# Identity products, three moves between engines and a new order in a pooled-attention and gated-MLP kernel

## The chip, the cores and the metric

The kernel runs on one core of a Trainium2 chip. The metric is the device time in microseconds, as the median of three runs. Five things work side by side on the core: TensorE (PE, with its weight loads as PEld), VectorE (DVE), ScalarE (ACT), GpSimd (POOL) and the DMA queue that SyncE (SP) feeds. Each engine takes its own instructions strictly in the order in which the program wrote them, and waits on semaphores for the others.

## The reference

Three layers follow one another. Batch is 8, with 8 heads, 576 positions and a head size of 64.

```python
def _attn_ref(q, k, v):
    k_p = k.reshape(B, H, S // 8, 8, D).mean(axis=3)      # pooled keys
    v_p = v.reshape(B, H, S // 8, 8, D).mean(axis=3)      # pooled values
    scores = scale * np.matmul(q, k_p.transpose(0, 1, 3, 2))
    scores = scores - np.max(scores, axis=-1, keepdims=True)
    attn = np.exp(scores)
    attn = attn / (np.sum(attn, axis=-1, keepdims=True) + 1e-09)
    return np.matmul(attn, v_p)

def _moe_ref(x, w_in, conv_w, w_out):                     # 512 -> 1024 -> 512
    h = np.maximum(x @ w_in, 0.0)
    conv_out = sum(conv_w[k] * shifted(h, k) for k in range(3))
    return (h * sigmoid(conv_out)) @ w_out

def _moe2_ref(x, w_in, g_ln, w_sg, b_sg, w_out):          # 512 -> 2 x 512 -> 512
    u, v = split(gelu_tanh(x @ w_in))
    v_n = (v - mean(v)) / np.sqrt(var(v) + 1e-06) * g_ln
    v_s = np.einsum('ts,bsd->btd', w_sg, v_n) + b_sg[None, :, None]
    return x + (u * v_s) @ w_out
```

## The kernel before

Every large product is computed from operands split into a high and a low part, each rounded for fast matmuls: three products per pair (high by high, low by high, high by low). The high part is written by ACT as a cast (`hi`), the low part by a subtraction in `subtract` (line 135), on DVE or POOL.

**What sets the order.** The work is written as small generators (`t_k`, `t_s`, `t_v2` and so on), and a long string `ORDER` lists which of them advances by one `yield` at each step. The function `step` also ties each instruction to the one before it on its engine, so the string alone fixes the order on all five queues. A token such as `s2.1` is task `s`, part 2, batch 1.

**The stages.** (1) The start, to about 55 us: the keys and values of batch 0 are loaded and pooled over eight rows, q is transposed through PE and an ACT copy (`qT`), the scores come from `KBT` (the pooled keys, L423), DVE takes the maximum and subtracts it (L434, L436), ACT does the exponential, DVE the sum and its reciprocal, POOL scales (`en`, L453, L457), PE transposes (L483, L492), ACT and DVE write the split parts `eTh` and `eTl`. The attention products (`t_a`, through `passes` at L776) read these and the pooled values `Vh`, `Vl`, `VR`, and ACT writes the rows `xh` and `xl` of the first MLP. Ident, the 128x128 identity, is made by POOL at the very start. (2) To about 540 us: hidden slices `t_i` (L106, twelve matmuls each into a `psi` bank, then ACT and DVE: L567, L577, L579, L580, L582, L586) and their output products `t_o`, with the attention of later batches between them. (3) To about 735 us: the input product of the second MLP in a form with seven products of quarter blocks instead of eight (`t_v2`, `t_u`, `t_xc`); `t_v2` ends with the normalisation of v (statistics on DVE, L813 and L814; 1/sqrt on POOL, L817 and L818; subtract and multiply on DVE, L821) and a store to `vs`. (4) To the end: per batch, `vs` is read back, sums and splits `sc` are made (POOL at L957, ACT at L626, DVE at L135), the remaining 64 rows become `vr` (L965), the spatial products `t_sp` run, DVE adds (L1006), POOL multiplies by u (L1010), and the last product `t_o2` (L99 to L101) adds the residual.

**Banks.** `psi` is a ring of two PSUM banks (`i_bank`), `psa` of three, `pso` of three. The two `psi` banks carry the hidden slices, the scratch of weight conversions (`to_f32`, L147, L150, L153) and the last products.

**Pooling the first keys.** `t_k(i, b)` pools blocks of 128 rows (two per step, 64 rows in the last). For batch 0, steps 0 and 2 are one DVE reduction each (L251), and step 1 is three additions on POOL (L253, L255, L257). `t_kfin` then transposes the five pooled blocks `kp` by PE (L294) into `KBT`.

Of the kernel before, what the change touches and what calls it, by code (L numbers as in the profile page):

```python
# [11 lines left out]
AF = mybir.ActivationFunctionType  # L12
ALU = mybir.AluOpType
# [13 lines left out]
def pooled_attention_gated_mlps(  # L27
# [23 lines left out]
    nc = tc.nc  # L51
# [15 lines left out]
    REM = S - NM * 128  # L67
# [24 lines left out]
    def i_bank():  # L92
        return psum1.tile([128, 512], F32, tag="i", bufs=2, name="psi")
# [40 lines left out]
    def subtract(out, in0, hi, eng=nc.vector):  # L134
        eng.tensor_tensor(out=out, in0=in0, in1=hi.bitcast(F32), op=ALU.subtract)  # L135
# [125 lines left out]
    def t_k(i, b):  # L261

        n = (2, 2, 1)[i]
        P = 128 if i < 2 else 64
        if b > 1:
            raw = att2.tile([128, 2, 512], F32, tag="raw", name="raw")
        else:
            raw = staged(f"st{b}", n, ((in1, "xh", XW * KC), (slot, "hg", 2 * NF * CH))[b] if i == 0 else None)
        rows_ = k[b].rearrange("h (j r) d -> (h j) (r d)", r=POOL)[256 * i:256 * i + P * n]
        nc.sync.dma_start(out=raw[0:P, 0:n], in_=rows_.rearrange("(a p) x -> p a x", p=P))  # L270
        if b == 1:
            kv["k1", i] = raw
        yield
        if b == 1:
            return
        if ("kp", b) not in kv:
            kv["kp", b] = att1.tile([128, 5, D], F32, tag="kp", name="kp")
        eng = dve if b == 0 and i != 1 else pool
        yield from pool_sum(eng, raw[:, 0:n], kv["kp", b][0:P, 2 * i:2 * i + n, :], P)
# [502 lines left out]
    def t_v2(a, k):  # L782
# [37 lines left out]
        for j in range(2):  # L820
            nc.vector.tensor_scalar(out=vg[:, j, :], in0=vg[:, j, :], scalar1=mv[:, j, 0:1], scalar2=rs[:, j:j + 1],  # L821
                                    op0=ALU.subtract, op1=ALU.mult)
# [108 lines left out]
    def t_w_out2(i, *_):  # L931
        p, tag = ((slot, "w4"), (slot, "w6"), (w2["q"], "T3"), (w2["q"], "T4"))[i]
        return weight(p, tag, w_out2[128 * i:128 * i + 128, :], dve, i_bank, lambda hl: wo2.__setitem__(i, hl))
# [28 lines left out]
    def t_vr(_, b):  # L962
        x = vf[b, 0][:, 2]
        r = vrs[b] = w2["p"].tile([128, HF], F32R, tag=f"b{1 + b % 2}", name="vr")
        nc.scalar.copy(out=r, in_=x)  # L965
        yield
        subtract(r[REM:128], x[REM:128], r[REM:128])
# [161 lines left out]
```

## Time and profile before

| what | us |
|---|---|
| three runs | 942.87, 940.72, 941.30 (median 941.3) |
| profiled execution: device time | 941.96 |
| profiled execution: span from the first to the last instruction | 940.2 |
| PE busy in the span | 915.5 (97%) |
| DVE busy | 757.6 (81%) |
| POOL busy | 558.0 (59%) |
| ACT busy | 534.6 (57%) |
| mean granted TensorE clock | 0.993 of full speed |

How to read it: a row of a timeline gives the start and the duration in us, the engine, the line of the kernel, the operation, the tile written and the tiles read, the shape and the count of merged instructions; in brackets stands the idle time of the engine just before it and what ended that. A row of windows gives a stretch, its length, the busy time and the number of instructions of PE, PEld, DVE, ACT and POOL, then the granted TensorE clock (1.00 is 2.4 GHz, 0.50 is 1.2 GHz), the busy share of the DMA engines and GB/s. A row of groups gives line, engine, operation, tiles and shapes, the count, and after the bar the busy time in us, the mean duration in ns, and the idle time before them with its releasers. PE's durations overlap, since matmuls are pipelined: the spacing of starts is the cost of one.

### The profile page before, as it was taken

Reading aid. Unit: us, or ns where it says so; the run is one execution under the profiler, and the core shown is the slowest. Engines: PE = TensorE matmul, PEld = TensorE weight load, DVE = VectorE, ACT = ScalarE, POOL = GpSimd, SP = SyncE. Lnnn points to the kernel's source line nnn. Section 1 sums busy time; section 2 is a strip of 40 time slices with the busy share of each in tenths; the row PEclk is TensorE's granted clock in tenths of the full one; section 3 lists DMA queues with packets and bytes.
Section 4 is the critical chain, followed back from the end, with each engine's and each line's share of the span. In section 5 each row is a group of like instructions: output and inputs, shape, how many; then the busy total and the mean of one; then the engine's idle time right before and its main releaser. Section 6 shows DMA issues by size and latency. Waiting matters only on the chain.

```text
span 940.2 us, 15870 instructions
## 1 busy us (share of the span) xinstructions
PE 915.5 (97%) x5412; PEld 839.1 (89%) x5412; DVE 757.6 (81%) x1383; ACT 534.6 (57%) x1125; POOL 558.0 (59%) x630
## 2 busy tenths in 40 slices
PE   5899999999999999999999999999999999999998
PEld 4797889989898898998998899999999998998996
DVE  5789988888977697797688778898787988888764
ACT  3766777767767576667646657656666422323211
POOL 3686797886878666457326456643563654555421
PEclk9799999999999999999999999999999999999999
DMA  9974384755645535323353474556536745476644
GB/s 236 247 208 101 107 177 126 168 152 153 168 124 134 134 102 125 106 73 105 92 131 85 88 161 133 153 186 197 141 134 219 263 149 197 151 208 196 182 163 134
DMA packets 185901, 143.62 MB, mean 153 GB/s; under 512 B 106048, under 2 KB 140124, under 8 KB 185820
## 3 DMA queue, kind: packets, MB, share of 16 engines
q1 hardware_dynamic: 185820, 142.61, 55.6%
q8 instruction: 42, 0.69, 0.3%
q14 instruction: 39, 0.32, 0.1%
HBM read 94.20 MB, written 48.37 MB: 152 GB/s over the span
## 4 chain that ended last, share of the span: by engine, by line
PE 86%; DVE 7%; ACT 2%; DMA 2%; issue 1%; SPq 0%; POOL 0%; DVEq 0%; ACTq 0%; POOLq 0%
PE psi L106 21%; PE psa L776 17%; PE pso L776 13%; PE pso L99 7%; PE pso L101 7%; PE pso L100 7%; PE psa L423 4%; PE psi L101 3%; PE psi L99 3%; PE psi L100 3%; PE psa L106 1%; DMA vf<-vs 1%; DVE sc L135 1%; DVE mx L434 1%; DMA q<-in_q_dram 1%
## 5 line engine op out<-in xcount | busy, mean ns | idle before, releaser
L135 POOL TENSOR_TENSOR hg<-g,hg 128x384 fp32r<-128x384 f32 x96 | 99.9, 1049 | 70.7 <-ACT hg L589 69.8
L1010 POOL TENSOR_TENSOR u<-u,tmp 128x288 f32<-128x288 f32 x64 | 60.4, 966 | 61.5 <-DVE tmp L1006 61.3
L579 DVE SCALAR_TENSOR_TENSOR psi<-h,coef,psi 128x384 f32<-128x384 f32 x96 | 58.9, 614 | 37.6 <-ACT psi L577 37.0
L582 ACT ACTIVATE psi<-psi 128x384 f32<-128x384 f32 x96 | 45.8, 478 | 51.9 <-DVE psi L580 51.5
L567 ACT ACTIVATE h<-psi 128x386 f32<-128x386 f32 (+1 forms) x96 | 47.4, 494 | 47.7 <-PE psi L106 47.3
L717 POOL TENSOR_TENSOR xb<-xb 128x768 f32<-128x768 f32 x24 | 45.4, 1892 | 43.6 <-DVE xc L135 27.6
L135 POOL TENSOR_TENSOR eTl<-xb,eTh 128x512 fp32r<-128x512 f32 (+1 forms) x30 | 45.4, 1513 | 39.1 <-ACT eTh L507 31.1
L586 DVE SCALAR_TENSOR_TENSOR g<-psi,h 128x384 f32<-128x384 f32 x96 | 52.2, 546 | 14.8 <-ACT psi L582 12.8
L626 ACT CAST sc<-vf 128x512 fp32r<-128x512 f32 x48 | 28.9, 619 | 61.3 <-POOL vf L957 35.2
L580 DVE SCALAR_TENSOR_TENSOR psi<-h,coef,psi 128x384 f32<-128x384 f32 x96 | 59.8, 623 | 3.4
L589 ACT CAST hg<-g 128x384 fp32r<-128x384 f32 x96 | 48.0, 508 | 24.3 <-DVE g L586 24.1
L577 ACT ACTIVATE psi<-h,coef 128x384 f32<-128x384 f32 x96 | 56.3, 586 | 3.1
L423 PE MATMUL psa<-KBT,qT 128*128 128x144 f32 (+1 forms) x320 | 52.5, 296 | 3.0 <-ACT qT L405 1.3
L423 PEld LDWEIGHTS psa<-KBT,qT 128*128 128x128 f32 (+1 forms) x320 | 44.3, 182 | 10.1 <-issue 4.0
L776 PE MATMUL pso<-wc,xc 128*128 128x256 f32 x378 | 50.9, 283 | 1.0 <-ACT tmp L799 0.9
L776 PEld LDWEIGHTS pso<-wc,xc 128*128 128x128 f32 x378 | 48.5, 189 | 1.9 <-ACT tmp L799 1.6
L776 PE MATMUL psa<-wc,xc 128*128 128x256 f32 x378 | 50.0, 282 | 0.0
L776 PE MATMUL psa<-xc,wc 128*128 128x384 f32 x252 | 48.2, 338 | 0.9 <-ACT tmp L843 0.9
L776 PEld LDWEIGHTS psa<-wc,xc 128*128 128x128 f32 x378 | 48.4, 189 | 0.2
L776 PE MATMUL pso<-xc,wc 128*128 128x384 f32 x252 | 47.8, 337 | 0.0
L135 DVE TENSOR_TENSOR sc<-vf,sc 128x512 fp32r<-128x512 f32 x48 | 41.2, 869 | 8.0 <-ACT sc L626 8.0
L1025 ACT CAST g<-u 128x256 fp32r<-128x256 f32 x64 | 22.6, 403 | 42.3 <-POOL u L1010 39.3
(403 smaller groups left out, 3110.3 us busy)
## 6 DMA issues: line engine op xcount, KB each, us to landing
xb<-eds SPq DMA_DIRECT2D x24, 384.0 KB, 3.4
x2s<-ob SPq DMA_DIRECT2D x36, 256.0 KB, 2.3
us<-ub SPq DMA_DIRECT2D x24, 384.0 KB, 3.3
vs<-vg SPq DMA_DIRECT2D x18, 512.0 KB, 3.1
u<-us SPq DMA_DIRECT2D x16, 576.0 KB, 6.7
vf<-vs SPq DMA_DIRECT2D x16, 512.0 KB, 3.8
out_dram<-ob SPq DMA_DIRECT2D x32, 256.0 KB, 2.0
xb<-x2s SPq DMA_DIRECT2D x40, 192.0 KB, 4.1
```

Source lines behind the costliest of these rows:

```text
L99: nc.tensor.matmul(out=out_, lhsT=ah, rhs=bh, start=first, stop=False)
L100: nc.tensor.matmul(out=out_, lhsT=al, rhs=bh, start=False, stop=False)
L101: nc.tensor.matmul(out=out_, lhsT=ah, rhs=bl, start=False, stop=last)
L106: nc.tensor.matmul(out=out_, lhsT=a, rhs=b_, start=(i == 0), stop=(i == n - 1))
L135: eng.tensor_tensor(out=out, in0=in0, in1=hi.bitcast(F32), op=ALU.subtract)
L423: nc.tensor.matmul(out=ps[0:n, 2 * SP * x:2 * SP * x + 2 * SP], lhsT=qT[:, p, 0:n], rhs=KBT[:, p, :], start=True, stop=True)
L577: nc.scalar.activation(out=y, in_=tap(1), func=AF.Copy, scale=cw(1, f))
L579: nc.vector.scalar_tensor_tensor(out=y, in0=tap(0), scalar=cw(0, f), in1=y, op0=ALU.mult, op1=ALU.add)
L580: nc.vector.scalar_tensor_tensor(out=y, in0=tap(2), scalar=cw(2, f), in1=y, op0=ALU.mult, op1=ALU.add)
L586: nc.vector.scalar_tensor_tensor(out=go, in0=y, scalar=1.0, in1=tap(1), op0=ALU.add, op1=ALU.mult)
L776: nc.tensor.matmul(out=ps, lhsT=a, rhs=b_, start=first and i == 0, stop=last and i == n - 1, skip_group_check=True)
L1010: pool.tensor_tensor(out=z, in0=z, in1=o, op=ALU.mult)
```

## The change

Five things change. Lines after the first edit stand 3, 12 or more higher in the new kernel (L423 becomes L426, L776 becomes L779, L1010 becomes L1022).

1. In the pooling of batch 0's keys, step 1 is split: one of its two blocks is a DVE reduction, the other stays three additions on POOL, of half the size.
2. A new task `t_turn` (token X) takes a `psi` bank and multiplies the identity by itself; nothing reads the result. There are 37.
3. The subtractions of the four weights of the last product (`t_w_out2`), and those of `vr` for batches 0 and 1, go from DVE to POOL.
4. In the last block (k = 5) and for its second and third part, the normalisation runs on ACT as scale and bias, and POOL makes the bias in two more instructions on two columns. `t_v2` has one more `yield` for all parts.
5. `ORDER` is another list.

```diff
-ORDER = '''z k0.0 k1.0 k2.0 z z p0.0 c p1.0 ...
+ORDER = '''z k0.0 k1.0 k2.0 z z p0.0 c p1.0 ...
...
         eng = dve if b == 0 and i != 1 else pool
+        if b == 0 and i == 1:
+            yield from pool_sum(dve, raw[:, 1:2], kv["kp", b][:, 3:4, :], P)
+            n = 1
         yield from pool_sum(eng, raw[:, 0:n], kv["kp", b][0:P, 2 * i:2 * i + n, :], P)
...
-        for j in range(2):
-            nc.vector.tensor_scalar(out=vg[:, j, :], in0=vg[:, j, :], scalar1=mv[:, j, 0:1], scalar2=rs[:, j:j + 1],
-                                    op0=ALU.subtract, op1=ALU.mult)
+        if k == NBLK - 1 and a:
+            pool.tensor_tensor(out=mv[:, :, 0], in0=mv[:, :, 0], in1=rs, op=ALU.mult)
+            pool.tensor_scalar(out=mv[:, :, 0], in0=mv[:, :, 0], scalar1=-1.0, scalar2=None, op0=ALU.mult)
+            yield
+            for j in range(2):
+                nc.scalar.activation(out=vg[:, j, :], in_=vg[:, j, :], func=AF.Identity, scale=rs[:, j:j + 1],
+                                     bias=mv[:, j, 0:1])
+        else:
+            yield
+            for j in range(2):
+                nc.vector.tensor_scalar(out=vg[:, j, :], in0=vg[:, j, :], scalar1=mv[:, j, 0:1],
+                                        scalar2=rs[:, j:j + 1], op0=ALU.subtract, op1=ALU.mult)
...
-        return weight(p, tag, w_out2[128 * i:128 * i + 128, :], dve, i_bank, lambda hl: wo2.__setitem__(i, hl))
+        return weight(p, tag, w_out2[128 * i:128 * i + 128, :], pool, i_bank, lambda hl: wo2.__setitem__(i, hl))
...
-        subtract(r[REM:128], x[REM:128], r[REM:128])
+        subtract(r[REM:128], x[REM:128], r[REM:128], pool if b < 2 else dve)
...
+    def t_turn(*_):
+        ps = i_bank()
+        nc.tensor.matmul(out=ps[:, 0:128], lhsT=ident, rhs=ident, start=True, stop=True)
```

The new order shows at three places. The first is DVE at the start; `kp` is the pooled keys, `st` the loaded ones, `cf` the filter taps. Before:

```order
L251 TENSOR_REDUCE kp<-st_139 128x128
L251 TENSOR_REDUCE kp<-st_139 64x64
L147 TENSOR_SCALAR cf<-craw 24x128
L300 COPY KBT<-psa 64x3x72
L303 COPY KBT<-psa 64x64
```

Now:

```order
L251 TENSOR_REDUCE kp<-st_139 128x64
L251 TENSOR_REDUCE kp<-st_139 128x128
L251 TENSOR_REDUCE kp<-st_139 64x64
L147 TENSOR_SCALAR cf<-craw 24x128
L303 COPY KBT<-psa 64x3x72
L306 COPY KBT<-psa 64x64
```

The new reduction of the half block, whose keys are loaded second, stands ahead of the block that is loaded first.

The second is PE from the small products of the filter taps (L188) to the first attention product (L776, now L779), some 26 to 35 us into the run. Before:

```order
L188 MATMUL psa<-ident,cf 128x28
L106 MATMUL psa<-q_148,ident 64x64 x8
L401 MATMUL psa<-ident,q_148 128x64 x4
L483 MATMUL psa<-ident,en 128x128 x4
L423 MATMUL psa<-KBT,qT 64x144 x2
L492 MATMUL psa<-ident,en 32x128 x2
L401 MATMUL psa<-ident,qb 128x128 x4
L423 MATMUL psa<-KBT,qT 64x144 x2
L776 MATMUL psa<-eTh,Vh 128x288
```

Now:

```order
L106 MATMUL psa<-q_148,ident 64x64 x8
L1086 MATMUL psi<-ident 128x128 x3
L404 MATMUL psa<-ident,q_148 128x64 x4
L486 MATMUL psa<-ident,en 128x128 x4
L404 MATMUL psa<-ident,qb 128x128 x4
L1086 MATMUL psi<-ident 128x128
L426 MATMUL psa<-KBT,qT 64x144 x2
L495 MATMUL psa<-ident,en 32x128 x2
L1086 MATMUL psi<-ident 128x128
L426 MATMUL psa<-KBT,qT 64x144 x2
L1086 MATMUL psi<-ident 128x128 x2
L779 MATMUL psa<-eTh,Vh 128x288
```

The transposes of the next batch's q (`qb`) stand one group earlier, ahead of the scores that wait for `qT`, and seven identity products stand between the rest. Of the 37, eleven open PE's queue, fifteen lie between the first transposes and the end of the first attention products, one lies among the hidden slices, and ten lie where stage 3 turns into stage 4.

The third is POOL at that turn, near 739 to 753 us; `u` is the tile that t_sp multiplies, `vr` the 64 remaining rows, `T3hl` and `T4hl` two weights of the last product. Before:

```order
L957 TENSOR_TENSOR vf<-sf,vf 128x2x256
L1010 TENSOR_TENSOR u_8231<-u_8231,tmp_8565 128x288
L1010 TENSOR_TENSOR u_8581<-u_8581,tmp_8614 128x288
L1010 TENSOR_TENSOR u_8231<-u_8231,tmp_8673 128x288
L1010 TENSOR_TENSOR u_8581<-u_8581,tmp_8683 128x288
L1010 TENSOR_TENSOR u_8231<-u_8231,tmp_8565 128x288
L1010 TENSOR_TENSOR u_8581<-u_8581,tmp_8614 128x288
L957 TENSOR_TENSOR vf<-vf 128x2x256
```

Now:

```order
L1022 TENSOR_TENSOR u_8394<-u_8394,tmp_8695 128x288
L1022 TENSOR_TENSOR u_8441<-u_8441,tmp_8631 128x288
L1022 TENSOR_TENSOR u_8394<-u_8394,tmp_8738 128x288
L1022 TENSOR_TENSOR u_8441<-u_8441,tmp_8760 128x288
L1022 TENSOR_TENSOR u_8394<-u_8394,tmp_8695 128x288
L1022 TENSOR_TENSOR u_8441<-u_8441,tmp_8631 128x288
L135 TENSOR_TENSOR vr<-vf,vr 64x512
L1022 TENSOR_TENSOR u_8394<-u_8394,tmp_8714 128x288
L1022 TENSOR_TENSOR u_8441<-u_8441,tmp_8690 128x288
L135 TENSOR_TENSOR T4hl<-t,T4hl 128x512
L969 TENSOR_TENSOR vf<-vf 128x2x256
L135 TENSOR_TENSOR T3hl<-t,T3hl 128x512
```

Three subtractions have come between the products with u.

## Rows read from the trace of the kernel before

**Rows 1.** The page: busy us per engine; a group: count, busy us, mean ns.
```profile
PE 915.5 (97%) x5412; PEld 839.1 (89%) x5412; DVE 757.6 (81%) x1383; ACT 534.6 (57%) x1125; POOL 558.0 (59%) x630
...
L586 DVE SCALAR_TENSOR_TENSOR g<-psi,h 128x384 f32<-128x384 f32 x96 | 52.2, 546 | 14.8 <-ACT psi L582 12.8
```

**Rows 2.** Windows: length, busy us (count) of PE, PEld, DVE, ACT, POOL; clock; DMA.
```profile
80.00:100.00 20.00, 19.06 (x111) 15.84 (x110) 18.82 (x38) 14.72 (x34) 13.44 (x19) 1.00 0.61 143
...
720.00:740.00 20.00, 17.84 (x136) 17.04 (x135) 18.12 (x37) 9.95 (x21) 13.69 (x12) 1.00 0.85 275
```

**Rows 3.** Timeline of PE, its start: start us, us, line, operands, count [idle before].
```profile
8.89 1.09 PE L401 MATMUL psa<-ident,q 128*128 128x128 f32 x4 [8.89 <-DMA q<-in_q_dram]
9.77 1.30 PE L294 MATMUL psa<-ident,kp 128*64 128x128 f32 x5
...
14.21 0.63 PE L401 MATMUL psa<-ident,q 128*128 128x128 f32 x4
...
15.92 2.02 PE L106 MATMUL psa<-st,ident 128*128 128x128 f32 x16
```

**Rows 4.** Timeline of DVE and POOL, the pooling of batch 0's keys.
```profile
4.87 1.87 DVE L251 TENSOR_REDUCE kp<-st 128x128 f32<-128x1024 f32 x1 [3.26 <-DMA st<-in_k_dram]
...
6.88 1.26 POOL L253 TENSOR_TENSOR st<-st 128x512 f32<-128x512 f32 x1 [4.10 <-DMA st<-in_k_dram]
...
7.84 1.01 DVE L251 TENSOR_REDUCE kp<-st 64x64 f32<-64x512 f32 x1 [1.10 <-DMA st<-in_k_dram]
...
9.02 0.45 POOL L257 TENSOR_TENSOR kp<-st 128x128 f32<-128x128 f32 x1
```

**Rows 5.** Windows of 5 us where the granted clock falls.
```profile
25.00:30.00 5.00, 3.54 (x33) 2.91 (x33) 4.76 (x11) 3.97 (x14) 4.20 (x9) 0.98 1.10 236
30.00:35.00 5.00, 4.52 (x17) 3.32 (x18) 4.27 (x10) 3.34 (x8) 4.04 (x9) 0.50 1.11 176
35.00:40.00 5.00, 4.24 (x18) 3.54 (x16) 3.36 (x6) 2.92 (x7) 4.42 (x4) 0.50 1.11 216
```

**Rows 6.** Timeline of PE from 28 to 48 us.
```profile
30.48 1.22 PE L423 MATMUL psa<-KBT,qT 128*64 128x144 f32 x4 [1.28 <-ACT qT L405]
...
34.58 0.45 PE L776 MATMUL psa<-eTl,Vh 128*128 128x288 f32 x1
34.82 0.45 PE L776 MATMUL psa<-eTh,Vl 128*128 128x288 f32 x1
...
47.31 0.30 PE L776 MATMUL psa<-eTh,Vl 128*128 128x288 f32 x1
47.45 0.29 PE L776 MATMUL psa<-eTh,VR 96*128 96x288 f32 x1
```

**Rows 7.** Timeline of POOL, what gates the first attention products.
```profile
31.94 1.26 POOL L135 TENSOR_TENSOR VR<-vrm,VR 32x512 fp32r<-32x512 f32 x1 [0.71 <-ACT VR L367]
...
43.39 1.20 POOL L453 TENSOR_TENSOR en<-e,rs 64x256 f32<-64x256 f32 x2 [3.52 <-ACT xl L540]
```

**Rows 8.** Timeline of DVE in the third stage of batch 0.
```profile
98.29 1.30 DVE L408 STREAM_TRANSPOSE qT<-qb 128x512 f32<-128x512 f32 x2
```

**Rows 9.** Groups, 700 to 770 us: shapes, count, busy us, mean ns, idle before.
```profile
L821 DVE TENSOR_SCALAR vg<-vg,mv,rstd 128x512 f32<-128x512 f32 x10 | 5.0, 540 | 0.9 <-POOL rstd L818 0.9
...
L818 POOL TENSOR_TENSOR rstd<-rstd,small 128x2 f32<-128x2 f32 x5 | 4.3, 852 | 0.4
...
L808 ACT ACTIVATE vg<-vg 128x512 f32<-128x512 f32 x4 | 2.5, 633 | 2.6 <-DVE vg L804 2.6
...
L135 DVE TENSOR_TENSOR vr<-vf,vr 64x512 fp32r<-64x512 f32 x2 | 1.5, 756 | 0.1
```

**Rows 10.** Timeline of DVE near 750 us.
```profile
749.61 0.69 DVE L135 TENSOR_TENSOR T3hl<-t,T3hl 128x512 fp32r<-128x512 f32 x1 [0.20 <-ACT T3hl L211]
```

**Rows 11.** Timeline of PE, the longest wait after 120 us.
```profile
738.77 1.06 PE L776 MATMUL pso<-sgp,sc 128*128 128x288 f32 x6 [1.56 <-DVE tmp L1006]
```

**Rows 12.** Timeline of POOL in the same stretch.
```profile
738.84 6.45 POOL L1010 TENSOR_TENSOR u<-u,tmp 128x288 f32<-128x288 f32 x6
```

More of the change, by code (lines that the diff above doesn't have):

```diff
@@ L1069, in t_o2 @@
                 nc.sync.dma_start(out=out[r0:r0 + REM, :], in_=ob[REM * e:REM * e + REM])
-    tasks = {"z": t_setup, "c": t_coef, "i": t_w_in, "t": t_w_out, "k": t_k, "K": t_kfin, "v": t_v, "V": t_vfin,
+    def t_turn(*_):
+        ps = i_bank()
+        nc.tensor.matmul(out=ps[:, 0:128], lhsT=ident, rhs=ident, start=True, stop=True)
+    tasks = {"X": t_turn, "z": t_setup, "c": t_coef, "i": t_w_in, "t": t_w_out, "k": t_k, "K": t_kfin, "v": t_v, "V": t_vfin,
              "q": t_q, "p": t_qtr, "s": t_s, "e": t_e, "x": t_x, "h": t_hg, "a": t_a, "I": t_i, "O": t_o, "A": t_att_close,
```

2 lines of the change are left out of this document (1 added, 1 removed).

## The prediction

> **What bounds the kernel now.** I read the page first: PE is busy 915.5 of the 940.2 us of the span [rows 1], so nearly all of the time is PE's own queue, and a gain can only come from PE's idle time or from time in which its clock is low. I then went through the windows and the timeline of PE to see where either lies. There are four places.
>
> The first is the start. PE does nothing for 8.89 us, until the first q has landed, and its first products are slow: four transposes start at 8.89 and the next group at 9.77, 0.22 us each, against 0.63 us for four at 14.21 [rows 3]. The second is the stretch from 30 to 40 us. PE idles 1.46 us from 25 to 30 us, 1.28 of it in one gap that ends at 30.48 with ACT's copy of `qT`, and then the granted clock is 0.50, the lower of its two levels (1.2 GHz), for both of the next windows [rows 5, 6]. The same attention product goes from a spacing of 0.24 us (34.58 to 34.82) to one of 0.14 us (47.31 to 47.45) when the clock is back at 1.00 (2.4 GHz) [rows 6]. The third is the stretch behind it, where DVE is the full engine: from 80 to 100 us it is busy 18.82 of 20 us and PE idles 0.94 us [rows 2]. The fourth is the turn from stage 3 to stage 4: from 720 to 740 us PE idles 2.16 us, 1.56 of it in one wait for DVE's `tmp`, with DVE at 18.12 of 20 [rows 2, 11]. Between 120 and 600 us PE hardly idles, and the end of the program has the same tasks in the same sequence as before.
>
> **The change part by part.** The sums are made against the profiled execution (941.96 us); the median of the three runs is 0.66 us lower, and that is taken off at the end.
>
> *Pooling by halves.* POOL's three additions for two blocks run from 6.88 to 9.47 us [rows 4]. Half of that leaves POOL ready about a microsecond earlier. But DVE now takes the half block first, and its keys land at 6.88, when POOL could start [rows 4]; a block of 512 elements per row costs 1.01 us, the pair that DVE used to take at 4.87 costs 1.87, the last block 1.01 [rows 4]. DVE thus ends at 6.88 + 1.01 + 1.87 + 1.01 = 10.77, and the first pair is ready at 9.76, where the pooled-key transposes started at 9.77 anyway [rows 3]. Only the fifth transpose waits for 10.77, and the copy that everything waits for needs the first four. I take 0, with +0.6 as the bad end (the fifth transpose holds up the queue).
>
> *Eleven identity products ahead of the data.* A 128x128 product of this type costs 2.02 / 16 = 0.13 us at the high level [rows 3]. Eleven at the low level of 0.22 are 2.4 us, and need only the identity, so they end near 4 us, well before 8.89, and delay nothing. If they leave the clock high, the early groups gain: the two groups of four transposes 0.4 us each; at most 0.9 us. The row shows that after idleness PE begins slow [rows 3], and some five microseconds of idleness still lie between these products and the data. So I take 0, with -0.9 as the other end. The Trainium skill, "TensorE: Matmul & The Clock Gate" (Part 1, What's actually happening), says that the throttled state is the default, that activity releases it and that idleness brings it back; that speaks against these eleven. The trace agrees as far as it goes: the slow first products follow 8.89 us without work. By that page this term is 0, by the other reading -0.9.
>
> *Fifteen among the first tiles.* At 0.13 us they are 1.9 us. PE idles 2.70 us from 25 to 40 us alone (5 - 3.54, 5 - 4.52, 5 - 4.24) [rows 5], and the new order has seven of the fifteen there. Since they depend on nothing late they fill gaps; some will end up ahead of work that was ready. I take +0.4, between 0 and 1.9.
>
> *The clock from 30 to 40 us.* This is the main term. The three identity products and the transposes of `qb` (4 x 0.16 [rows 3]) now stand before the scores that waited until 30.48, so about 1.0 us of the gap that came just before the fall is filled. If the clock stays high, PE's 8.76 us of work in those two windows [rows 5] becomes 4.38: 4.4 us is the most. But POOL gates the first attention product with `VR`, which ends at 31.94 + 1.26 = 33.20 [rows 7] whatever the clock does. Of the ten microseconds 6.8 lie behind that; less the 0.76 idle of the second window, half of 6.0 is 3.0 us. What is late next is ACT, which writes each `xh` before the next product can go on, and I give 0.5 back for it. The scaled scores of the last tile can follow: POOL waited 3.52 us for them at 43.39 [rows 7], so POOL has room. I take -2.5, between 0 and -4.4.
>
> *The turn.* DVE loses the four normalisations of two parts (540 ns each, 2.2 us), two `vr` subtractions (756 ns each, 1.5) [rows 9] and, near 750 us, two weight subtractions (0.69 each, 1.4) [rows 10]: 5.1 us of an engine that is full there. PE's idle 2.16 us there [rows 2] is the most that this can return; I take 1.6, since some of it is PE's own chain. Ten identity products at 0.13 cost 1.3 on PE's queue there. Net -0.3, between +1.3 and -0.9. ACT takes the normalisations; the nearest row is a 128x512 activation of 633 ns [rows 9], so four are 2.5 us on an engine that is busy 9.95 of 20 us there [rows 2], and they feed rows that only the last two batches read: nothing on the path. Of the two subtractions moved that lie near 640 us, I take 0, since neither DVE nor POOL sets PE's pace there for long. POOL gets four subtractions of 512 columns (1.26 us each by the nearest row [rows 7]) and four small ones of at most 0.85 us each [rows 9]; what that can do is a rival.
>
> *The rest.* One identity product among the hidden slices: +0.13. The new order elsewhere: 0, from -0.9 (the idle of 80 to 100 us goes [rows 2]) to +2.7 (second rival). Sum: -2.5 + 0.4 + 0.1 - 0.3 = -2.3; 941.96 - 2.3 - 0.66 = **939.0 us**.
>
> **The rivals.** *The clock falls all the same, one step later.* With the gap before 30.48 filled, the next thin place is the one ahead of `VR`: two groups of scores (1.22 us each at the low level [rows 6], 0.6 at the high), two small transposes and four identity products until 33.20, some 2.0 us of work in 2.7. If the clock falls there, it is low for the attention products just as before, and the main term is 0: 941.96 + 0.4 + 0.1 - 0.3 - 0.66 = 941.5. For it speaks that POOL's queue up to `VR` has the same instructions in the same sequence in both orders; against it that the work that stood before the fall was thinner still.
>
> *DVE work pulled ahead: slower.* In the new order DVE has 190 instead of 187 instructions ahead of the filter taps of the eleventh hidden slice: one more pooling (1.01 us [rows 4]), one more transpose of q (1.30 / 2 = 0.65 [rows 8]) and one more gating product (0.55 [rows 1]); at the third slice it is two maxima and two subtractions more. The difference is 2.2 us there and up to 2.7 with the shapes that changed, and nearly gone by the fifteenth. DVE is full in that stretch and PE already waits for it [rows 2]. It decides as soon as DVE's queue reaches 60 us without having gained as much as it was given; if the clock term is lost too, the whole sum is 941.96 + 0.2 + 2.7 - 0.66 = 944.2.
>
> *POOL binds at the turn.* POOL multiplies six times without a break from 738.84 to 745.29 [rows 12]; the second `vr` stands behind these six, then the two weights. By my count PE reaches the products with that `vr` about when POOL ends it (745.3 + 1.3), so each microsecond that POOL comes late is one that PE waits. Then the gain of 1.6 is gone: 939.0 + 1.6 = 940.6. The Trainium skill, "GPSIMD Engine Reference" (section 4.1, Engine selection), advises against two-input elementwise work on GpSimd as about half as fast as VectorE. The rows agree: 1.26 against 0.69 to 0.76 us for 512 columns [rows 7, 9, 10].
>
> *More than forecast.* The clock is high from the first data on (-0.9), the whole 3.0 is kept, the idle of 80 to 100 us goes (-0.9) and the turn gives its best (-0.9): 941.96 - 5.7 + 0.1 - 0.66 = 935.7.
>
> **How the numbers follow.** The forecast gets 0.43, the later fall 0.23, DVE 0.13, the larger gain 0.13, POOL 0.08. The forecast's own range is 937.0 to 940.4. The range that should hold 8 in 10 runs from 935.0, a little under the larger gain, to 943.0, which leaves most of the DVE rival out. About 0.2%, 1.9 us, is what a measurement of this kernel can tell from no change. Faster than 939.4: 0.38 of the forecast, all of the larger gain and a little of the later fall, 0.55. Slower than 943.2: 0.11 of DVE and 0.03 of the later fall, 0.14. The rest, 0.31, is the same.
>
> **What would show it.** In the windows after, the granted clock from 30 to 45 us: 1.00 throughout makes the main term right, 0.50 from about 33 us makes the first rival right. The first transposes near 8.9 us: four in 0.9 us or in 0.6. The first hidden slice should start 2 to 3 us earlier than before. PE's idle from 60 to 120 us tells whether DVE gave the gain back. From 720 to 740 us, PE's wait for `tmp` should be gone and no wait for POOL in its place. The prediction is wrong if PE idles somewhere between 120 and 700 us, where I counted the new order at nothing.

## The result: 0.95% slower, and the profile after

| | median us | runs | ratio to the kernel before, 95% interval |
|---|---|---|---|
| kernel before, beside it | 942.09 | 4 (940.72 to 943.89) | 1 |
| changed kernel | 950.98 | 4 (950.44 to 952.19) | 1.0095 [1.0074, 1.0116] |

The forecast was 939.0 us, with a range to 943.0. The profiled execution of the changed kernel took 952.19 us, its span 950.4.

The page of the changed kernel, busy time by engine (to set against [rows 1]):

```profile
PE 928.1 (98%) x5486; PEld 852.7 (90%) x5486; DVE 758.9 (80%) x1374; ACT 539.4 (57%) x1129; POOL 565.8 (60%) x640
```

PE's idle time is smaller than before: 950.4 - 928.1 = 22.3 us against 940.2 - 915.5 = 24.7. But the eleven products now fill part of the wait at the start: up to its first transposes PE idles 3.1 us (1.38 + 1.72) where it idled 8.89 [rows 3]. Behind them it idles 19.2 us against 15.8. The rest of the loss is in PE's *busy* time: 74 more matmul records (37 products, two records each), and products that run at half speed. Windows of the changed kernel (length, busy us and count of PE, PEld, DVE, ACT, POOL, granted clock, DMA share, GB/s); the first three answer to [rows 5]:

```profile
25.00:30.00 5.00, 4.36 (x43) 3.83 (x42) 4.79 (x9) 4.20 (x15) 4.04 (x10) 1.00 1.10 213
30.00:35.00 5.00, 4.63 (x34) 3.75 (x33) 4.16 (x10) 4.22 (x9) 4.19 (x6) 1.00 1.10 220
35.00:40.00 5.00, 2.40 (x18) 1.93 (x18) 1.13 (x3) 1.80 (x6) 4.08 (x7) 0.99 1.07 214
40.00:47.00 7.00, 7.00 (x41) 6.45 (x40) 5.57 (x10) 3.19 (x12) 1.45 (x3) 0.52 1.06 373
...
115.00:120.00 5.00, 3.18 (x14) 3.18 (x15) 3.71 (x7) 1.81 (x4) 3.15 (x4) 0.84 0.88 214
120.00:125.00 5.00, 4.50 (x17) 4.15 (x16) 3.07 (x7) 4.06 (x10) 1.98 (x3) 0.50 0.15 52
```

The clock is at 1.00 from 30 to 40 us (0.99 in the second half), where the kernel before had 0.50: that part of the forecast came true. But there are two new holes, 35 to 40 us (PE busy 2.40 of 5) and 115 to 120 us (3.18 of 5), and behind each of them the clock is at its lower level for some 7 us.

How far the changed kernel is behind can be read from start times: for every product that both traces have with the same operands, its start after less its start before. The medians by place of the trace before, for the kernels of this document (one trace of each, worked out from the rows of PE; in us, negative is ahead):

| place, us | 20-40 | 40-60 | 60-80 | 100-120 | 120-140 | 200-220 | 320-340 | 340-360 | 700-720 | 760-780 |
|---|---|---|---|---|---|---|---|---|---|---|
| changed kernel | -0.3 | 2.1 | 2.5 | 2.7 | 7.0 | 7.0 | 7.8 | 9.1 | 9.3 | 10.6 |
| e4, without products | -0.3 | 2.0 | 2.3 | 2.4 | 5.3 | 5.4 | 6.2 | 7.5 | 7.1 | 7.4 |
| e3, two entries moved | -0.2 | -3.2 | -0.9 | -0.8 | -1.0 | -0.9 | -0.1 | 1.2 | 1.1 | 2.2 |
| e5, e3 without products | 0.0 | -3.3 | -1.4 | -1.6 | -1.6 | -1.5 | -0.7 | 0.6 | 0.2 | 1.0 |
| e9, e5 with four more moved | 0.0 | -2.9 | -1.2 | -1.1 | -1.1 | -1.1 | -1.3 | -0.8 | -1.1 | -1.2 |
| e7, before with the moved work | -0.2 | -2.3 | -2.1 | -2.1 | -2.1 | -2.1 | -2.3 | -2.3 | -2.3 | -0.3 |
| e12, before with products in its waits | -0.5 | -2.5 | -2.4 | -2.3 | -2.3 | -2.3 | -2.5 | -2.5 | -2.6 | -2.2 |

Seven of the nine microseconds are lost by 130 us, in two steps that sit behind the two holes. Here is the first hole: one row of POOL in the kernel before, then rows of POOL, ACT and PE of the changed kernel:

```profile
29.34 0.11 POOL L519 MEMSET xl<- 128x8 f32 x1
```

```profile
34.06 1.30 POOL L135 TENSOR_TENSOR wi1hl<-t,wi1hl 128x512 fp32r<-128x512 f32 x1
35.31 1.29 POOL L135 TENSOR_TENSOR wi0hl<-t,wi0hl 128x512 fp32r<-128x512 f32 x1
36.55 1.27 POOL L253 TENSOR_TENSOR raw<-raw 128x512 f32<-128x512 f32 x1
37.75 0.12 POOL L522 MEMSET xl<- 128x8 f32 x1
37.79 0.12 POOL L523 MEMSET xl<- 128x8 f32 x1
...
37.90 0.41 ACT L543 ACTIVATE xl<-psa 128x288 fp32r<-128x288 f32 x1 [2.90 <-POOL xl L523]
...
38.37 0.39 PE L495 MATMUL psa<-ident,en 128*32 128x128 f32 x2 [2.20 <-ACT xl L543]
```

POOL clears the edges of `xl` in two instructions of 0.12 us. In the kernel before they stand ahead of `VR` (31.94 [rows 7]). In the new order they stand behind it, and behind two weight subtractions and a pooling step, 3.9 us of work; the first product that reads one of these weights starts at 56.28. ACT may not write the first `xl` until they are done (2.90 us idle), and PE waits for ACT (2.20 us). The second hole, PE and then DVE:

```profile
114.54 0.39 PE L779 MATMUL psa<-xh,minus 128*128 128x288 f32 x1
116.82 0.44 PE L106 MATMUL psi<-xh,wi1hl 128*128 128x388 f32 x1 [1.90 <-DVE g L589]
...
113.38 0.64 DVE L153 SCALAR_TENSOR_TENSOR t<-w6raw,psi 128x512 uint32<-128x512 uint32 x1
...
116.22 0.55 DVE L589 SCALAR_TENSOR_TENSOR g<-psi,h 128x384 f32<-128x384 f32 x1
116.69 0.68 DVE L147 TENSOR_SCALAR psi<-w7raw 128x512 uint32<-128x512 uint32 x1
```

There are two `psi` banks. The conversion of weight w6 gives one back at 114.02 (113.38 + 0.64). The order writes the conversion of w7 ahead of the hidden slice wi1, so w7 gets that bank, though it doesn't start before 116.69, and the slice has to wait for the other bank, which `g` frees at 116.77.

### The profile page after: what moved, and what is told of

Same layout as the page of the kernel before. It is cut to its first block, busy times and chain, and to the rows that moved or that the text cites. A ratio compares the mean times of both kernels' runs of the same rounds, so it can differ in the third digit from the quotient of the medians.

```text
span 950.4 us, 16018 instructions
## 1 busy us (share of the span) xinstructions
PE 928.1 (98%) x5486; PEld 852.7 (90%) x5486; DVE 758.9 (80%) x1374; ACT 539.4 (57%) x1129; POOL 565.8 (60%) x640
## 4 chain that ended last, share of the span: by engine, by line
PE 79%; DVE 7%; DMA 4%; POOL 2%; ACT 2%; SPq 2%; issue 2%; POOLq 0%; DVEq 0%; ACTq 0%
PE psi L106 20%; PE psa L779 14%; PE pso L779 12%; PE pso L99 6%; PE pso L101 6%; PE pso L100 6%; PE psi L101 3%; PE psi L99 3%; PE psi L100 3%; PE psa L426 3%; DMA st<-in_v_dram 2%; DMA qb<-in_q_dram 1%; SPq L270 1%; DVE vg L833 1%; DMA vf<-vs 1%
## 5 line engine op out<-in xcount | busy, mean ns | idle before, releaser
L1022 POOL TENSOR_TENSOR u<-u,tmp 128x288 f32<-128x288 f32 x64 | 58.8, 937 | 69.8 <-DVE tmp L1018 46.3
L779 PE MATMUL pso<-wc,xc 128*128 128x256 f32 x378 | 51.5, 283 | 1.7 <-DVE vg L807 1.0
L779 PEld LDWEIGHTS pso<-wc,xc 128*128 128x128 f32 x378 | 48.6, 189 | 3.1 <-DVE vg L807 1.7
L426 PE MATMUL psa<-KBT,qT 128*128 128x144 f32 (+1 forms) x320 | 51.1, 291 | 0.0
L779 PE MATMUL psa<-wc,xc 128*128 128x256 f32 x378 | 50.1, 281 | 0.2 <-ACT tmp L802 0.2
L464 POOL TENSOR_TENSOR en<-e,rs 128x512 f32<-128x512 f32 (+1 forms) x30 | 32.0, 1066 | 29.6 <-DVE rs L451 13.5
L426 PEld LDWEIGHTS psa<-KBT,qT 128*128 128x128 f32 (+1 forms) x320 | 44.1, 181 | 6.0 <-issue 2.2
L779 PEld LDWEIGHTS psa<-wc,xc 128*128 128x128 f32 x378 | 48.3, 189 | 0.4 <-ACT tmp L802 0.4
L779 PE MATMUL psa<-xc,wc 128*128 128x384 f32 x252 | 48.2, 338 | 0.0
L779 PE MATMUL pso<-xc,wc 128*128 128x384 f32 x252 | 47.9, 337 | 0.0
```

Of the source, the lines that this page charges most:

```text
L426: nc.tensor.matmul(out=ps[0:n, 2 * SP * x:2 * SP * x + 2 * SP], lhsT=qT[:, p, 0:n], rhs=KBT[:, p, :], start=True, stop=True)
L779: nc.tensor.matmul(out=ps, lhsT=a, rhs=b_, start=first and i == 0, stop=last and i == n - 1, skip_group_check=True)
L1022: pool.tensor_tensor(out=z, in0=z, in1=o, op=ALU.mult)
```

## Experiments

Each ratio is to runs of the kernel before on the same chip. Theory 1 is that the new order's own stalls carry the loss.

**e1: the edges of `xl` cleared earlier.**

```diff
-... s4.0 s4.0 s4.0 V.0 V.0 v1.1 V.0 ... k0.2 i6 i2 X23 x1 X6 a1.0 a1.0
+... s4.0 s4.0 s4.0 V.0 x1 V.0 v1.1 V.0 ... k0.2 i6 i2 X23 X6 a1.0 a1.0
```

> The changed kernel with one entry of its order moved: the clearing of the edges of xl (two GpSimd memsets of 0.12 us) stands between the low halves of V and the mask product, some 8 us earlier than in the changed kernel, where it stood behind two low halves of weights and a pooling step and ScalarE's first xl waited 2.90 us for it. Theory 1 (the new order's own stalls carry the loss, each with a stretch of low clock behind it): the wait of TensorE at 38.37 us (2.20 us) goes, the clock doesn't fall at 39.87 us, so the 6.83 us at half speed give back 3.4 us; together 5.6 us, 945.4 us (943.5 to 947.5). Theory 2 (the TensorE queue is short of other work there, and the wait goes to the next link, the low halves and the eT copies): the idle time comes back within the same 10 us and the time stays at 949 to 951 us.

Measured: 946.1 us, 1.0049 [1.0032, 1.0067]: 0.46% or 4.3 us less than the changed kernel's ratio, three quarters of what theory 1 gave. In its trace the memsets stand at 29.11 us and the clock doesn't fall at 40 us:

```profile
35.00:40.00 5.00, 4.80 (x44) 4.10 (x43) 3.71 (x7) 3.96 (x12) 4.12 (x6) 1.00 1.07 205
40.00:45.00 5.00, 4.45 (x39) 4.12 (x39) 3.91 (x8) 3.45 (x13) 2.45 (x4) 1.00 1.04 358
...
113.43 0.44 PE L106 MATMUL psi<-xh,wi1hl 128*128 128x388 f32 x1 [1.90 <-DVE g L589]
```

Theory 2 falls. The second hole is still there, as long as before, but in this trace the clock stays at 1.00 behind it (115 to 120 us).

**e2: the slice ahead of the weight conversion.**

```diff
-... s1.2 I0.1 I0.1 t7 t7 a3.1 t6 I0.1 I1.1 I0.1 t7 a0.1
+... s1.2 I0.1 I0.1 I1.1 t7 t7 a3.1 t6 I0.1 I0.1 t7 a0.1
```

> The changed kernel with one entry of its order moved: the products of the second tile's second hidden slice (weights wi1) are written ahead of the splitting of weight w7, so that the slice and not the split takes the PSUM bank which the split of w6 gives back at 114.0 us; the order of VectorE is the same. Theory 1: the slice starts at about 114.95 us instead of 116.82, the waits of 1.90 and 0.5 us go, the clock doesn't fall at 118.38 us (6.83 us at half speed, worth 3.4 us): 5 to 6 us off, 945.4 us (944 to 948). Theory 2 (the bank is only the nearest of several limits; VectorE and ScalarE are late there as a whole): the slice starts earlier, and the wait reappears at the next slice; 949 to 951 us.

Measured: 947.93 us, 1.0070 [1.0051, 1.0090]: 0.25% or 2.4 us less. The windows of its trace beside those of the changed kernel:

```profile
115.00:120.00 5.00, 4.46 (x27) 3.98 (x26) 4.76 (x9) 3.80 (x9) 3.50 (x6) 1.00 0.79 201
120.00:125.00 5.00, 5.00 (x29) 4.60 (x28) 4.59 (x11) 4.62 (x11) 4.32 (x8) 1.00 0.51 143
```

The wait for the bank is gone, with the same order on DVE, and the clock stays up in this execution. The gain is that of the idle time (1.9 and a little); the 3.4 us that I had added for the clock don't show in the median. The trace of e1, where the clock stays up behind this very wait, shows that the second fall doesn't come in every execution. The granted clock of its runs (0.991 to 0.996) is hardly above that of the changed kernel's (0.990 to 0.993).

**e3: both.**

> The changed kernel with both entries moved. Theory 1: the two gains add up, 951.0 less 11.2 us is 939.8 us (937.5 to 943), which is the time that the prediction gave for the change. Theory 2: 948 to 951 us. If one stall only uncovers the other's limit, the gain of both is less than the sum of the two single ones.

Measured: 943.57 us, 1.0024 [1.0013, 1.0035]. The gain, 0.71%, is the sum of the two single ones (0.46 and 0.25). So the two misplaced entries are 6.7 us of the 8.9 that were lost. It is just outside the range of theory 1: what is left is still slower than before.

**e4: without the 37 products, the stalls left in.**

> The changed kernel without the 37 unread products of the identity; everything else, and the order of the rest, is the same. Theory 1 (the order's two stalls carry the loss, the products only cost their own time): the 22 behind the head that stand in TensorE's way give back at most 26 x 0.14 = 3.6 us, and the clock then falls earlier in the gap near 30 us, as in the kernel before, which takes up to 3.4 us back: 947.5 to 952 us. Theory 3 (the products are the loss, by their time, or because each takes one of two PSUM banks in turn): 940 to 943 us, and the waits at 38 and 116 us are gone with them.

Measured: 949.0 us, 1.0084 [1.0060, 1.0107]. The products are not what made the kernel slow; both holes are still there (2.18 us at 38, 2.06 us at 117). Theory 1 had the clock fall near 30 us without them; in this trace it does, for some 3 us:

```profile
30.00:35.00 5.00, 4.42 (x21) 2.73 (x19) 3.76 (x9) 3.50 (x9) 4.19 (x6) 0.74 1.13 232
```

**e5: e3 without the 37 products.**

> The changed kernel with both entries of its order moved and without the 37 unread products. It asks whether the products hold TensorE's clock. Theory 1 (they do, between 28 and 36 us): without them the clock falls again between 25 and 40 us, which costs 3 to 5 us, and their own time, about 26 x 0.14 = 3.6 us behind the head, comes back: 942 to 945 us, and rows at half speed stand between 28 and 46 us. Theory 2 (the mended order alone holds the clock): no fall behind 14 us, and the time is 943.6 - 3.6 = 940.0 us.

Measured: 941.96 us, 0.9996 [0.9986, 1.0005]. Windows of its trace:

```profile
25.00:30.00 5.00, 3.65 (x36) 3.03 (x36) 4.79 (x10) 4.33 (x16) 4.26 (x12) 1.00 1.09 218
30.00:35.00 5.00, 3.74 (x24) 2.52 (x22) 4.36 (x10) 4.11 (x10) 4.20 (x6) 1.00 1.11 230
35.00:40.00 5.00, 4.52 (x39) 3.64 (x38) 3.56 (x8) 3.80 (x11) 4.18 (x6) 1.00 1.08 183
```

PE idles more than in the kernel before in the second window (1.26 us against 0.48 [rows 5]), a little less in the other two, and keeps its clock. One trace settles little here, since that of e4, which lacks the same products, has 0.74. But the granted clocks of the eleven runs have a median of 0.999, against 0.994 for the kernel before beside them. So theory 1 of this run falls: in the mended order the products are not needed to hold the clock in most executions. They cost 0.28%, 2.6 us; theory 2 had 3.6.

**e6: e3 without the ten products at the turn.**

> The changed kernel with both entries moved and without the ten unread products at the turn between the two stages (735 to 760 us). Theory 1 (each stands in a full queue and costs its own 0.14 us, and the wait for tmp there goes on): 1.0 to 1.4 us off, 942.4 us (941.8 to 943.0), with a wait of 0.7 to 1.6 us for tmp near 736 us and the clock at 1.00 from 720 to 760 us. Theory 2 (they fill the wait for tmp and hold the clock over it): no gain, 943.6 us, or a loss of up to 3.4 us where the clock falls.

Measured: 943.66 us, 1.0019 [1.0007, 1.0031], against 1.0024 for e3: within the intervals. By the ratios the ten products cost 0.5 us, less than the 1.0 to 1.4 us I gave them, but the intervals don't exclude 1.4. PE's longest wait for `tmp` is 1.71 us here and 1.12 in e3. That they stand partly in this wait isn't shown by it: the load that the wait hangs on (see e7) also took 0.4 us longer here.

**e7: the kernel before with the moved work and its own order.** The pooled halves, the low halves on GpSimd and the normalisations on ScalarE, with the two `yield`s that the change added taken out again (the diff is against the changed kernel):

```diff
         if k == NBLK - 1 and a:
             pool.tensor_tensor(out=mv[:, :, 0], in0=mv[:, :, 0], in1=rs, op=ALU.mult)
             pool.tensor_scalar(out=mv[:, :, 0], in0=mv[:, :, 0], scalar1=-1.0, scalar2=None, op0=ALU.mult)
-            yield
             for j in range(2):
...
         else:
-            yield
             for j in range(2):
```

> The kernel before, in its own order, with the changed places of the work alone: the pooled block of keys in halves on VectorE and GpSimd, the small low halves and those of the second output weights on GpSimd, the last normalisations on ScalarE (with their GpSimd step in the step before, so that the order's entries stay the same). Theory 1 (5 us less on VectorE at the turn don't move the wait of 1.56 us for tmp, which hangs on another link): 941.5 us within 0.9. Theory 2 (the prediction's: the wait goes): 939.5 to 940.2 us.

Measured: 942.98 us, 1.0009 [0.9995, 1.0022]. By the ratio theory 1 holds: the moved work gains nothing (a cost of up to 2 us isn't excluded). The turn shows why. One window and two rows of the kernel before, then the same of e7 with PE's and DVE's rows:

```profile
720.00:745.00 25.00, 22.84 (x174) 22.04 (x173) 23.12 (x46) 10.36 (x22) 18.69 (x17) 1.00 0.86 291
...
727.59 1.68 SPq L940 DMA_DIRECT2D vf<-vs  x2
...
734.15 0.62 ACT L626 CAST sc<-vf 128x512 fp32r<-128x512 f32 x1 [3.55 <-DMA vf<-vs]
```

```profile
720.00:745.00 25.00, 22.49 (x158) 21.85 (x158) 20.54 (x39) 12.23 (x23) 19.07 (x23) 0.93 0.85 274
...
725.27 2.12 SPq L950 DMA_DIRECT2D vf<-vs  x2
...
733.04 0.62 ACT L629 CAST sc<-vf 128x512 fp32r<-128x512 f32 x1 [0.51 <-DMA vf<-vs]
...
733.69 1.20 DVE L135 TENSOR_TENSOR sc<-vf,sc 128x512 fp32r<-128x512 f32 x1 [1.68 <-ACT sc L629]
...
736.65 1.30 PE L779 MATMUL pso<-sgp,sc 128*128 128x288 f32 x6 [2.02 <-DVE tmp L1016]
```

DVE is relieved by 2.6 us in this stretch (23.12 to 20.54), and PE still waits, 2.02 us against 1.56 [rows 11]. DVE *idles* 1.68 us within that time: its next instruction, the low half `sc`, needs ACT's cast, and that needs the rows `vf`, whose load was issued by 727.4 and is used at 733.04. The `tmp` that PE waits for are queued on DVE behind this `sc`.

The longer wait need not be the change's doing. In e12 (below) the turn is that of the kernel before, with DVE not relieved:

```profile
724.93 1.68 SPq L940 DMA_DIRECT2D vf<-vs  x2
...
731.92 0.62 ACT L626 CAST sc<-vf 128x512 fp32r<-128x512 f32 x1 [3.92 <-DMA vf<-vs]
...
736.54 1.06 PE L776 MATMUL pso<-sgp,sc 128*128 128x288 f32 x6 [1.98 <-DVE tmp L1006]
```

From the issue to the cast it is 6.99 us here (731.92 - 724.93) and 6.56 in the trace before (734.15 - 727.59): the load took 0.43 us longer, and PE waited 0.42 us longer, in one and the same order of the turn. The trace of e7 loses 2.0 us over the turn (-2.3 to -0.3 in the table); of that the wait is 0.5, and behind it the clock is at its lower level for some 3 us (0.93 in the window).

**e11: loads behind the store.** e7 with three loads put off, to make room for that of `vf`:

```diff
-... R0.1 m2.1 y0.4 l2 d1.0 ... S2.1 l3 d0.0 ... d1.0 n1.5 D3.0 d1.1 l2 d0.1 l3
+... R0.1 y0.4 d1.0 ... S2.1 d0.0 ... d1.0 n1.5 m2.1 l2 l3 D3.0 d1.1 l2 d0.1 l3
```

> The kernel before with the changed places of the work, with three loads at the turn (the residual rows and the raw second output weights T3 and T4, 2 + 2 transfers) put behind the store of vg in SyncE's queue, some 3 us later, where the DMA engines are full (share 1.0 from 730 to 738 us). Theory 1 (the wait of 2.0 us at 734.6 us hangs on the load of vf, which takes about 6 us to land because the engines share it with these): vf lands 1 to 1.5 us earlier, the wait falls to 0.5 to 1.2 us, ratio 0.9985 to 0.9995. Theory 2 (vf goes through in the queue's order, and what follows doesn't slow it): the wait stays at 2.0, ratio 1.0005 to 1.0015.

Measured: 941.96 us, 1.0000 [0.9987, 1.0012]: not to be told from e7, and between the ranges of the two theories. In the trace:

```profile
726.85 2.12 SPq L950 DMA_DIRECT2D vf<-vs  x2
...
734.84 1.19 DVE L135 TENSOR_TENSOR sc<-vf,sc 128x512 fp32r<-128x512 f32 x1 [1.25 <-ACT sc L629]
737.79 1.06 PE L779 MATMUL pso<-sgp,sc 128*128 128x288 f32 x6 [1.58 <-DVE tmp L1016]
```

From the issue's start to DVE's `sc` it is 7.99 us (734.84 - 726.85) where e7 had 8.42 (733.69 - 725.27): 0.43 us sooner, and PE's wait is 0.44 us shorter. The two go together, as they should if the wait hangs on the load. But 0.43 us is also what the load differs by between the trace before and that of e12, with nothing changed at the turn. So that other loads slow this one isn't shown; what makes up its time was not tried.

**e8: the mended head on the old order.** The order of e3 up to 126 us, then the rest of the order before, with the moved work and without the ten late products.

> The mended order (both entries moved, with its 27 products) for the first 126 us, and from there the order of the kernel before, with the changed places of the work and without the products at the turn. The mended kernel is 1.1 us ahead of the kernel before between 140 and 180 us, and loses 3 us behind that. Theory 1 (what it loses is the new order's: waits of 0.75 and 1.16 us at 308 and 333 us, and the products at the turn): 940.4 us (939.5 to 941.5), faster than both kernels. Theory 2 (the gain of the head is given back wherever the order comes from): 941.5 to 944 us.

Measured: 945.96 us, 1.0040 [1.0026, 1.0054]. Both theories fall in their numbers, by the slower side. In the trace the head isn't 1.1 us ahead at 140 us but 1.3 behind; the lower clock stands once more, near 62 us, behind a wait of 1.27 us for `KBT` at 58.9; and the turn costs 2.2 us with a wait of 2.22. The run mixes three things and tells them apart badly; of the question it was made for it says little.

**e9: four more entries moved.** e5, each time one entry put ahead of what stood before it:

```diff
-... K.1 s0.1 t1 t1 I1.0 h I0.0 ...
+... K.1 I1.0 s0.1 t1 t1 h I0.0 ...
-... K.2 s3.1 e2.1 a0.1 ...
+... K.2 e2.1 s3.1 a0.1 ...
-... q.6 e1.5 I0.6 I0.6 s3.5 ...
+... q.6 I0.6 e1.5 I0.6 s3.5 ...
-... I4.6 a3.5 I4.6 I5.6 a3.5 ...
+... I4.6 I5.6 a3.5 I4.6 a3.5 ...
```

> The mended order without the 37 products, with four more entries moved, each at one of the waits of TensorE that are left in it: the second hidden slice (wi1) of the first tile ahead of the scores that wait for KBT (0.93 us at 58.5), VectorE's low half of eT ahead of a sum that isn't urgent (0.93 us at 90.7), VectorE's product g ahead of another low half of eT (0.76 us at 307.4), a hidden slice (wi5) ahead of the attention product that waits for its bank (1.16 us at 332.7). Theory 1 (what the new order lost in the stages counted at nothing is these single waits, each an entry or two too late): 3.8 us off the 941.4 us that the kernel without products takes beside this before, 0.9996 of it: ratio 0.9955 to 0.997, about 938.5 us. Theory 2 (each wait goes to the next link): ratio 0.9985 to 1.000.

Measured: 940.36 us, 0.9983 [0.9975, 0.9992], faster than both kernels, but 0.13% (1.2 us) below e5 where theory 1 gave 0.25% or more: just outside theory 2's range, and further from that of theory 1. The two later moves did what theory 1 said. Windows from 300 to 340 us in e5, then in e9:

```profile
300.00:320.00 20.00, 19.24 (x97) 16.87 (x96) 14.95 (x26) 12.44 (x21) 14.90 (x16) 1.00 0.69 164
320.00:340.00 20.00, 18.84 (x109) 17.40 (x109) 15.04 (x29) 12.86 (x30) 12.83 (x17) 1.00 0.22 66
```

```profile
300.00:320.00 20.00, 20.00 (x102) 17.70 (x101) 15.54 (x27) 12.52 (x22) 15.17 (x16) 1.00 0.71 168
320.00:340.00 20.00, 19.83 (x116) 18.30 (x115) 15.06 (x30) 13.28 (x31) 12.89 (x17) 1.00 0.24 70
```

The two earlier ones went to the next link, as theory 2 said; PE of e9 waits there for other things:

```profile
63.77 0.41 PE L404 MATMUL psa<-ident,qb 128*128 128x128 f32 x2 [1.27 <-issue]
...
92.98 0.66 PE L486 MATMUL psa<-ident,en 128*128 128x128 f32 x4 [1.46 <-POOL en L456]
```

**e10: only the eleven products ahead of the data.** e3 with the other 26 left out.

> The changed kernel with both entries moved and with only the eleven products that stand ahead of the data. Theory 1 (they run while TensorE has nothing else, and the higher clock of the first transposes is lost again in the fall at 9 to 13 us): the time of the kernel without any, ratio 0.999 to 1.0005. Theory 2 (they gain 0.9 us by the faster first tile): ratio 0.9985 or less. Theory 3 (they cost by what they make the clock do at 9 to 13 us): ratio 1.001 to 1.002.

Measured: 941.79 us, 1.0003 [0.9991, 1.0015]; e5, without any, has 0.9996. No gain, and no cost that can be told. The start of PE in e10, then in e5:

```profile
1.38 5.06 PE L1086 MATMUL psi<-ident 128*128 128x128 f32 x22 [1.38 <-POOL ident masks.py:199]
8.21 1.12 PE L404 MATMUL psa<-ident,q 128*128 128x128 f32 x4 [1.77 <-DMA q<-in_q_dram]
```

```profile
8.16 1.09 PE L404 MATMUL psa<-ident,q 128*128 128x128 f32 x4 [8.16 <-POOL e L433]
```

In these two traces the first four transposes take 1.1 us with the eleven and without; other traces with the eleven differ (see below). (This is also e3 against e10: the 26 other products cost 0.21%, 2.0 us.)

**e12: the kernel before with 18 products in its waits.** The task is added, and 5, 2, 3 and 8 entries X go into the order ahead of the four products that PE waits for between 21 and 30.5 us:

```diff
-... e1.0 e1.0 ... s3.0 i6 ... v2.0 i1 ... s4.0 s3.0 ...
+... X13 X14 X15 X16 X17 e1.0 e1.0 ... X11 X12 s3.0 i6 ... X8 X9 X10 v2.0 i1 ... X0 X1 X2 X3 X4 X5 X6 X7 s4.0 s3.0 ...
```

> The kernel before with 18 of the unread products put into its four waits of TensorE between 21 and 30.5 us (5, 2, 3 and 8; 0.87, 0.36, 0.50 and 1.28 us), and nothing else. Theory 1 (a full TensorE queue there holds the clock, whatever fills it, as the prediction had it): no fall at 29.8 us, mean low time from 11 us to under 4 us, 2 to 4 us off: ratio 0.996 to 0.998. Theory 2 (the clock falls for another reason, the products delay the work behind them by what they overhang): ratio 0.9995 to 1.001, and the low stretch stays.

Measured: 939.89 us, 0.9985 [0.9971, 0.9998], faster than before. Its windows, against [rows 5]:

```profile
25.00:30.00 5.00, 5.00 (x48) 4.48 (x47) 4.76 (x10) 3.95 (x15) 4.09 (x9) 1.00 1.10 258
30.00:35.00 5.00, 4.07 (x29) 3.08 (x27) 3.94 (x10) 3.39 (x8) 4.16 (x9) 1.00 1.11 185
35.00:40.00 5.00, 4.58 (x38) 3.82 (x38) 4.62 (x8) 4.52 (x11) 3.90 (x4) 1.00 1.11 236
```

Theory 1 holds for the clock: 0.50 has become 1.00, and nothing else was touched. Its time doesn't reach the range: 0.15% (1.4 us) where 0.2 to 0.4% was given, and the interval comes close to 1. The 18 products take 5.0 us of PE's queue in waits of 3.0 us. From the granted clocks of the eleven runs, the time at the lower level, (1 - clock) x 2 x span, has a median of about 2 us, against 7.5 in the runs of the kernel before beside them.

## Why the prediction was wrong

**The step that failed** is the last term of the sum: "The new order elsewhere: 0, from -0.9 ... to +2.7". It measured 6.7 us in two places (e3) and over a microsecond in others (e9, 1.2 us). With the two entries moved and the 26 products behind the head left out, the kernel takes 1.0003 of the time before (e10): the two entries (0.71%) and these products (0.21%) account for the loss. I had compared the orders engine by engine, counted what DVE got more, and judged the rest by how full an engine is. Neither hole comes from a full DVE: at the first it is busy 1.13 of 5 us, and the second goes in e2, where DVE's order is the same. The first is a tiny instruction that stands late on POOL. I had written, in the first rival, that POOL's queue up to `VR` has the same instructions in the same sequence in both orders. That is wrong: in the kernel before the memsets of `xl` stand ahead of `VR`, at 29.34, and in the new order behind it, at 37.75. A comparison of the two queues up to the first write of `xl` would have shown the move. The second is a bank that goes to whoever is *written* first, not to whoever can use it first. The sentence on what would make the prediction wrong (PE idling behind 120 us where the new order was counted at nothing) named the right term, but both holes lie ahead of that, at 36 and 115 us.

**The clock from 30 to 40 us, -2.5**: the mechanism is borne out on the order before (e12), the size is not. With the stalls out, e3 and e5 are 3.2 and 3.3 us ahead of the kernel before at 40 to 60 us. But that is set against one execution, whose clock is low for 10 us: e7, in the old order and without products, is 2.3 us ahead there too, where its clock is low for only some 3. Over the runs, e12's gain is 1.4 us. Two more things were not in the term. More than half is given back at once: PE comes earlier to the first scores of batch 1 and waits 0.93 us (e5) or 1.64 us (e3) for `KBT`. And it is not the products' doing in this order (e5). That a fuller queue ahead of 30 us does hold the clock is shown by e12, on the order before.

**Fifteen products, +0.4**: too low. The 26 products behind the head cost 2.0 us (e3 against e10), the ten late ones some 0.5 of that (e6), so these cost about 1.5 us, with intervals of about a microsecond on either number. The price was wrong as well: 2.02 / 16 = 0.13 us is that of one record, and a product of this type leaves two (the changed kernel has 74 for its 37). So each costs about twice what the sum says; e12's 18 take 5.0 us, 0.28 each. At that price fifteen are over 4 us, beyond the bad end, and the greater part of them did fill gaps. The same price stands in the terms for the eleven and the ten, and as 0.14 in what was expected of e4, e5 and e6.

**Eleven products, 0**: right in size (e10), by a reason that the traces bear out only in part. I had taken 0 by the reading that the five microseconds of idleness ahead of the data bring the low clock back. The Trainium skill, "TensorE: Matmul & The Clock Gate" (Part 1, What's actually happening), says that idleness does so; of the traces here, one of seven agrees for the first group. By the doubled price the eleven take 4.7 to 5.1 us and not 2.4, so that only 1.5 to 2.1 us of idleness lie behind them and not five. Without the eleven the four transposes take 1.09 us in the kernel before [rows 3] and in e5. With them they take 1.12 us in e10, but 0.65 or 0.66 in the other six traces, that of the changed kernel among them, and the next four were slow again there:

```profile
1.38 4.79 PE L1086 MATMUL psi<-ident 128*128 128x128 f32 x22 [1.38 <-POOL ident masks.py:199]
7.89 0.66 PE L404 MATMUL psa<-ident,q 128*128 128x128 f32 x4 [1.72 <-DMA q<-in_q_dram]
...
10.43 1.11 PE L404 MATMUL psa<-ident,q 128*128 128x128 f32 x4
```

The granted clock of the changed kernel is 1.00 from 5.8 to 9.1 us and 0.50 from 9.2 to 12.5. So in most traces the eleven do hand a high clock to the first group, worth 0.4 us on it, and in the changed kernel it is lost again within 3 us; in the time of e10 no gain can be told.

**The turn, -0.3**: not borne out in its parts. By the ratios e6 and e7 together give +1.3 us, with intervals that still hold -0.3, so the sum can't be called right or wrong. The relief of DVE (-1.6) is 0 (e7). I had read "waits for DVE's `tmp`" and "DVE busy 18.12 of 20" as one fact; but `tmp` is late because the load of `vf` is. In the changed kernel the wait is still there, 8.8 us later and 0.3 us shorter:

```profile
744.80 1.14 ACT L629 CAST sc<-vf 128x512 fp32r<-128x512 f32 x2 [4.93 <-DMA vf<-vs]
...
747.61 1.07 PE L779 MATMUL pso<-sgp,sc 128*128 128x288 f32 x6 [1.24 <-DVE tmp L1018]
```

ACT's idle 3.55 us before the same cast, for the same load, could have been read in the trace before. The ten products (+1.3) cost about 0.5 us (e6). POOL as the new bound, the third rival, didn't come about: POOL multiplies in the same 6.45 us as before [rows 12], and PE has no wait for it there. On its price the Trainium skill, "GPSIMD Engine Reference" (section 4.1), was borne out: the `vr` subtraction takes 1288 ns on POOL where DVE took 756 [rows 9].

**What stays open**: what makes up the time of the load of `vf` at the turn, and so what would take PE's wait there away; and why e9's first two moves only shifted their waits.

**Pooling by halves, 0**: e7, which has it, gives no difference.

**The rivals.** The one that ended on the slower side, DVE work pulled ahead, has the right sign and the right part of the program, and another mechanism: DVE is not the full engine (1.13 of 5 us at 35 to 40, 3.71 of 5 at 115 to 120). The later fall of the clock did come, near 40 us and not at 33, and behind a stall of its own.

## What to carry to other kernels

Where a change brings a new order, look in each queue for the small instructions that open something (a memset of an edge, the claim of a bank or a tile), and ask who cannot start without them: what an engine's load says about its room says nothing of these. When a wait is put down to an engine, follow it one step further back: an engine that is late because it waits itself is not relieved by taking work from it. Fillers that keep the clock up can pay where they stand in a real wait and the clock falls without them (e12: 18 of them, 1.4 us gained); the changed kernel's 26 cost 2 us, in an order that kept its clock without them in most executions.

## What the runs showed of the hardware

The same kernel gets a different clock from run to run, and its time goes with it: 14 runs of the kernel before on one chip had a mean granted clock of 0.992 to 0.998 and took 939.5 to 944.0 us; the six at 0.997 and over took 939.5 to 941.4, the four at 0.992 from 942.95 to 944.0. A single trace therefore shows one draw: e7's has the lower clock for some 3 us near 31 us where the trace before has it for 10, with the same products on PE in the same order up to there. A term that rests on the clock wants a median over runs, not the difference of two traces. And idleness alone doesn't tell whether the clock falls: in the trace of e5 PE idles 1.35 us of the 5 before 30 us and 1.26 of the 5 behind it and keeps its clock; in that of the kernel before it idles 1.46 us of the first 5 [rows 5] and then falls to half speed. What tells the two apart was not found.
